# Scores of two heads by 64-row matmuls in two halves of the TensorE array, without zero-padded copies

## The chip, the cores and the metric

The kernel runs on one core of a Trainium2 chip. The metric is the device time of one execution in microseconds (us). Ratios are the mean time of one kernel's fast runs over that of the kernel before in the same rounds, so they are not quite the ratio of the medians quoted beside them.

## The reference, cut to what matters

```python
# 4 sequences, 8 heads, 768 tokens, head dimension 48
for t in range(S):
    cur = einsum('bhd,bhe->bhde', u * k_t, v_t)
    y[:, :, t] = einsum('bhd,bhde->bhe', r_t, state + cur)
    state = w * state + einsum('bhd,bhe->bhde', k_t, v_t)
# then: x = y as [batch, token, head*dim]; each token goes to one of 8 experts
# (768x384 per sequence, hidden size 1024, relu), scaled by its gate
```

The recurrence is computed in chunks of 128 tokens. Inside a chunk, the term between tokens s < t is a score (r_t w^t)(k_s w^-(s+1)); what came before the chunk enters through a state. All data are float32.

## The kernel before

Two heads form a pair and fill the 128 partitions as 2 x 64 rows (48 of data, 16 of padding). There are 16 pairs: 4 sequences of 4. For a pair, `first` computes the state increments (`ds`), the scores (`sc`) and the token's own term (`dp`); `second`, which follows one pair later, computes the output (`yp`). At each fourth pair, `finish` turns the outputs (`tp`) and computes the logits (`lp`, `lq`).

```python
DP = 64                # rows that a head takes
rbs = [once.tile([P, NCH, 2, P], F32, name=f"rb{i}") for i in range(2)]   # zeroed in the other head's part
...
# first(n, hp, t)
nc.gpsimd.tensor_mul(rw, t["rT"], spread(pw[:, hp, :P], 1, NCH))
for i in range(2):                                    # the padded copies
    q = slice(i * DP, (i + 1) * DP)
    nc.scalar.copy(rb[q, :, i, :], rw[q])
nc.vector.tensor_mul(kw, t["kT"], spread(inv[:, hp], 1, NCH))
nc.gpsimd.tensor_mul(ke, t["k"], spread(endT[:, hp], 1, NCH))
nc.gpsimd.tensor_mul(pd, t["rT"], t["kT"])
ds = [bank("ds") for _ in range(2)]                   # 5 matmuls 128x128x128
...
for c in range(NCH - 1):                              # the state chain: VectorE, head by head
    for i in range(2):
        ...                                           # copy for c == 0, else state = w^128 state + ds
for g in range(0, NCH, 2):                            # scores
    sc = bank("sc")
    for c in range(2):
        nc.tensor.matmul(sc[:, c * 2 * P:(c + 1) * 2 * P], lhsT=kw[:, g + c, :],
                         rhs=rb[:, g + c].rearrange("p i t -> p (i t)"), start=True, stop=True)
    nc.vector.tensor_mul(am[:, g:g + 2]..., sc..., spread(mask, 1, 4))
...                                                   # dp and own; second() comes one pair later
```

`rw`, `kw`, `ke`, `pd`, `am` and `own` have two buffers each; all PSUM tiles go round through eight banks.

## Time and profile before

| | us |
|---|---|
| median of the runs before the prediction | 600.85 |
| attention (to the last logits) | 213 |
| routing and experts | 386 |
| one sequence of four pairs | 49.0 |

How the pairs are bounded is read in the prediction. Besides the lines there, three groups of the page matter: line, engine, operation, count, then busy us, mean ns, and the idle time of the engine before it with what ended it.

```profile
L138 PE MATMUL sc<-rb,kw 128*128 128x256 f32 x192 | 48.7, 406 | 22.7 <-ACT rb L112 22.7
...
L112 ACT COPY rb<-rw 64x768 f32<-64x768 f32 x32 | 26.6, 831 | 122.1 <-POOL rw L109 121.8
...
L140 DVE TENSOR_TENSOR am<-sc,mask 128x512 f32<-128x512 f32 x48 | 32.8, 691 | 9.9 <-PE sc L138 9.0
```

The 96 score matmuls are 192 records, since a float32 matmul is two. They hold TensorE for 48.7 us, and half of the products are with zeros. The 22.7 us of idle time ahead of them are the wait for the ScalarE copies.

### The profile page before, as it was taken

To read this page: it belongs to the slowest core of one execution; us is meant where nothing else is said; L and a number is where in the kernel's file an instruction comes from. 1 tells how busy PE (TensorE), PEld (TensorE's weight loads), DVE (VectorE), ACT (ScalarE), POOL (GpSimd) and SP (SyncE) were. 2 spreads that over 40 slices of the span, in tenths; PEclk is the share of its full clock that TensorE was granted. 3 is DMA by queue.
4 is the path that set the end of the run, shared out by engine and by line. 5 is a ranking of instruction groups with operands and counts; after the bars stand their busy time and mean duration, and the time that the engine had idled before them with its cause. 6 is when DMAs were issued, how large, how long until landed. Compare 5 with 4: busy or idle time off the path is not lost. (4 is left out here: it accounts for less than half of the span.)

```text
span 599.1 us, 8255 instructions
## 1 busy us (share of the span) xinstructions
PE 527.1 (88%) x3283; PEld 415.3 (69%) x3283; DVE 187.8 (31%) x433; ACT 79.6 (13%) x128; POOL 162.6 (27%) x140
## 2 busy tenths in 40 slices
PE   0888898898797933699999999999999999999994
PEld 0766656657666712588787887877878878778783
DVE  6796647738736347001101110111011101110010
ACT  1121211131222100011011010110110101101010
POOL 5964526434622011311121211211112112110010
PEclk9998999999999975599999999999999999999998
DMA  8686464654420115658999999988989899998830
GB/s 303 244 288 214 159 208 155 241 161 155 127 85 28 36 47 217 254 187 310 332 332 310 329 323 341 319 321 323 332 325 321 318 335 303 337 324 324 313 127 0
DMA packets 28411, 145.39 MB, mean 243 GB/s; under 512 B 4336, under 2 KB 7439, under 8 KB 20432
## 3 DMA queue, kind: packets, MB, share of 16 engines
q1 hardware_dynamic: 20448, 128.98, 61.2%
q0 software_dynamic: 3968, 10.82, 4.8%
q10 hardware_dynamic: 3952, 5.00, 2.3%
q8 instruction: 28, 0.46, 0.3%
q14 instruction: 15, 0.12, 0.1%
HBM read 135.35 MB, written 10.81 MB: 244 GB/s over the span
## 5 line engine op out<-in xcount | busy, mean ns | idle before, releaser
L490 PEld LDWEIGHTS hps<-exT,w1t 128*128 128x128 f32 x1488 | 173.0, 194 | 9.0 <-DVE exT L481 1.1
L490 PE MATMUL hps<-exT,w1t 128*128 128x128 f32 x1488 | 173.3, 277 | 0.6 <-DVE exT L481 0.6
L498 PE MATMUL eyp<-w2t,hT 128*128 128x384 f32 x496 | 165.1, 486 | 0.0
L498 PEld LDWEIGHTS eyp<-w2t,hT 128*128 128x128 f32 x496 | 91.8, 190 | 57.5
L492 ACT ACTIVATE hT<-hps 128x512 f32<-128x512 f32 x62 | 37.0, 597 | 331.4 <-PE hps L490 331.4
L502 POOL DMA_INDIRECT out_dram<-yo,sid x31 | 31.2, 1007 | 174.8 <-DVE yo L501 174.8
L138 PE MATMUL sc<-rb,kw 128*128 128x256 f32 x192 | 48.7, 406 | 22.7 <-ACT rb L112 22.7
L481 DVE COPY exT<-etp 128x384 f32<-128x384 f32 x31 | 17.3, 558 | 160.4 <-PE etp L479 160.4
L501 DVE TENSOR_SCALAR yo<-eyp,gate 128x384 f32<-128x384 f32 x31 | 19.1, 618 | 148.1 <-PE eyp L498 148.1
L471 POOL DMA_INDIRECT xg<-x_d,gid x31 | 30.6, 987 | 121.8 <-PE etp L479 107.3
L138 PEld LDWEIGHTS sc<-rb,kw 128*128 128x128 f32 x192 | 37.5, 202 | 30.4 <-ACT rb L112 25.3
L115 POOL TENSOR_TENSOR pd<-rT,kT 128x768 f32<-128x768 f32 x16 | 35.7, 2233 | 49.4 <-PE dp L148 38.0
L112 ACT COPY rb<-rw 64x768 f32<-64x768 f32 x32 | 26.6, 831 | 122.1 <-POOL rw L109 121.8
L130 DVE SCALAR_TENSOR_TENSOR st<-st,pw,ds 64x64 f32<-64x64 f32 x128 | 35.9, 280 | 4.1
L109 POOL TENSOR_TENSOR rw<-rT,pw 128x768 f32<-128x768 f32 x16 | 27.2, 1703 | 35.2 <-PE yp L159 35.2
L140 DVE TENSOR_TENSOR am<-sc,mask 128x512 f32<-128x512 f32 x48 | 32.8, 691 | 9.9 <-PE sc L138 9.0
L114 POOL TENSOR_TENSOR ke<-k,endT 128x768 f32<-128x768 f32 x16 | 29.1, 1818 | 6.2 <-DVE endT L93 3.0
L165 PE MATMUL yp<-am,v 128*64 128x128 f32 x384 | 29.3, 281 | 0.0
L120 PE MATMUL ds<-v,ke 128*128 128x128 f32 x160 | 23.1, 294 | 3.0 <-POOL ke L114 3.0
L159 PEld LDWEIGHTS yp<-rw,st 128*128 128x128 f32 x160 | 21.2, 191 | 6.2 <-issue 2.9
L159 PE MATMUL yp<-rw,st 128*128 128x128 f32 x160 | 25.1, 288 | 0.0
L120 PEld LDWEIGHTS ds<-v,ke 128*128 128x128 f32 x160 | 20.2, 200 | 6.1 <-POOL ke L114 3.4
(130 smaller groups left out, 278.5 us busy)
## 6 DMA issues: line engine op xcount, KB each, us to landing
w1t<-in_w_dram SPq DMA_DIRECT2D x31, 1536.0 KB
w2t<-in_w_dram SPq DMA_DIRECT2D x31, 1536.0 KB
rT<-in_rT_dram SPq DMA_DIRECT2D x16, 384.0 KB
kT<-in_kT_dram SPq DMA_DIRECT2D x16, 384.0 KB
k<-in_k_dram SPq DMA_DIRECT2D x16, 384.0 KB
v<-in_v_dram SPq DMA_DIRECT2D x16, 384.0 KB
vT<-in_vT_dram SPq DMA_DIRECT2D x16, 384.0 KB
x_d<-x ACTq DMA_DIRECT2D x4, 1152.0 KB
```

The source lines that it names most:

```text
L115: nc.gpsimd.tensor_mul(pd, t["rT"], t["kT"])
L120: nc.tensor.matmul(ds[c // 3][:, c % 3 * P:(c % 3 + 1) * P], lhsT=ke[:, c, :], rhs=t["v"][:, c, :], start=True, stop=True)
L130: nc.vector.scalar_tensor_tensor(state[q, c, i], state[q, c - 1, i], pw[q, hp, P:P + 1], add, Alu.mult, Alu.add)
L138: nc.tensor.matmul(sc[:, c * 2 * P:(c + 1) * 2 * P], lhsT=kw[:, g + c, :], rhs=rb[:, g + c].rearrange("p i t -> p (i t)"), start=True, sto ...
L140: nc.vector.tensor_mul(am[:, g:g + 2].rearrange("p c i t -> p (c i) t"), sc.rearrange("p (x t) -> p x t", t=P), spread(mask, 1, 4))
L159: nc.tensor.matmul(yp[:, c % 3 * P:(c % 3 + 1) * P], lhsT=t["state"][:, c - 1].rearrange("p i e -> p (i e)"), rhs=t["rw"][:, c, :], start= ...
L165: nc.tensor.matmul(yp[i * DP:(i + 1) * DP, c % 3 * P:(c % 3 + 1) * P], lhsT=t["v"][:, c, i * DP:(i + 1) * DP], rhs=t["am"][:, c, i, :], st ...
L471: nc.gpsimd.indirect_dma_start(out=xg, out_offset=None, in_=x_d, in_offset=bass.IndirectOffsetOnAxis(ap=gid[:, j:j + 1], axis=0))
L490: nc.tensor.matmul(hps[:, m * P:(m + 1) * P], lhsT=t[j]["w1"][:, 4 * g + m, kk, :], rhs=t[j]["xT"][:, kk, :], start=(kk == 0), stop=(kk == ...
L492: nc.scalar.activation(hT[:, 4 * g:4 * g + 4].rearrange("p m t -> p (m t)"), hps, Act.Relu)
L498: nc.tensor.matmul(yp[:, :D], lhsT=t[j]["hT"][:, m, :], rhs=t[j]["w2"][:, m, :], start=(m == 0), stop=(m == FK - 1))
L502: nc.gpsimd.indirect_dma_start(out=out, out_offset=bass.IndirectOffsetOnAxis(ap=sid[:, j:j + 1], axis=0), in_=yo, in_offset=None, bounds_c ...
```

## The change

The intent is to stop multiplying zeros. Each head's scores come from its own 64 rows, in its half of the array, so that both run at once; then no padded copy of `rw` is needed.

```diff
-        rbs = [once.tile([P, NCH, 2, P], F32, name=f"rb{i}") for i in range(2)]
...
-        for z in rbs + sts:
+        for z in sts:
...
-            for i in range(2):
-                q = slice(i * DP, (i + 1) * DP)
-                nc.scalar.copy(rb[q, :, i, :], rw[q])
...
-            t["am"] = am = two.tile([P, NCH, 2, P], F32, name="am")
-            for g in range(0, NCH, 2):
-                sc = bank("sc")
-                for c in range(2):
-                    nc.tensor.matmul(sc[:, c * 2 * P:(c + 1) * 2 * P], lhsT=kw[:, g + c, :],
-                                     rhs=rb[:, g + c].rearrange("p i t -> p (i t)"), start=True, stop=True)
-                nc.vector.tensor_mul(am[:, g:g + 2].rearrange("p c i t -> p (c i) t"),
-                                     sc.rearrange("p (x t) -> p x t", t=P), spread(mask, 1, 4))
+            t["am"] = am = two.tile([P, 2, NCH, P], F32, name="am")
+            for g in range(0, NCH, 3):
+                sc = [bank("sc") for _ in range(2)]
+                for c in range(3):
+                    for i in range(2):
+                        q = slice(i * DP, (i + 1) * DP)
+                        nc.tensor.matmul(sc[i][:, c * P:(c + 1) * P], lhsT=kw[q, g + c, :],
+                                         rhs=rw[q, g + c, :], start=True, stop=True)
+                for i in range(2):
+                    nc.vector.tensor_mul(am[:, i, g:g + 3], sc[i][:, :3 * P].rearrange("p (c t) -> p c t", t=P),
+                                         spread(mask, 1, 3))
...
-                                         lhsT=t["v"][:, c, i * DP:(i + 1) * DP], rhs=t["am"][:, c, i, :],
+                                         lhsT=t["v"][:, c, i * DP:(i + 1) * DP], rhs=t["am"][:, i, c, :],
```

More of the change, by code (lines that the diff above doesn't have):

```diff
@@ L106, in first @@
             pd = two.tile([P, NCH, P], F32, name="pd")
-            rb, state = rbs[n % 2], sts[n % 2]
+            state = sts[n % 2]
             t.update(rw=rw, state=state)
             nc.gpsimd.tensor_mul(rw, t["rT"], spread(pw[:, hp, :P], 1, NCH))
-            for i in range(2):
-                q = slice(i * DP, (i + 1) * DP)
-                nc.scalar.copy(rb[q, :, i, :], rw[q])
             nc.vector.tensor_mul(kw, t["kT"], spread(inv[:, hp], 1, NCH))
```

## The prediction

> **What bounds the kernel now.** I read the page first (busy shares, then the 40 slices). The kernel has two stages: attention up to 213 us, experts from about 235 us on. The change touches attention alone, so I cut the trace into stretches by time.
>
> ```profile
> PE 527.1 (88%) x3283; PEld 415.3 (69%) x3283; DVE 187.8 (31%) x433; ACT 79.6 (13%) x128; POOL 162.6 (27%) x140
> ```
>
> TensorE leads overall, but that is an average over both stages. The stretches below are one whole sequence (four pairs of heads) and two single pairs, from one `ds` block to the next:
>
> ```profile
> 83.06:132.08 49.02, 42.52 (x288) 31.74 (x287) 31.10 (x73) 10.24 (x16) 23.29 (x13) 1.00 0.55 185
> 132.08:141.82 9.74, 8.38 (x63) 6.77 (x61) 7.72 (x18) 1.66 (x2) 5.51 (x4) 1.00 0.39 123
> 141.82:152.00 10.18, 8.38 (x63) 6.77 (x61) 7.72 (x18) 1.66 (x2) 5.95 (x4) 1.00 0.49 164
> ```
>
> The columns are PE, weight loads, VectorE, ScalarE, GpSimd, clock, DMA share, GB/s. A pair takes 10.18 us, TensorE works 8.38 us of it and VectorE 7.72: TensorE is the bound, VectorE is close behind, DMA and ScalarE are far from it. The 1.80 us in which TensorE rests are one wait, which the view of waits of TensorE for the stage shows and the timeline explains:
>
> ```profile
> PE sc L138 <- ACT rb L112: 22.7, 14, 2.0
> ...
> PE ds L120 <- POOL ke L114: 3.0, 1, 3.0
> ```
>
> ```profile
> 141.41 1.83 POOL L109 TENSOR_TENSOR rw<-rT,pw 128x768 f32<-128x768 f32 x1
> ...
> 141.82 1.38 PE L120 MATMUL ds<-v,ke 128*128 128x128 f32 x10
> ...
> 143.27 1.67 ACT L112 COPY rb<-rw 64x768 f32<-64x768 f32 x2 [8.51 <-POOL rw L109]
> ...
> 145.00 2.86 PE L138 MATMUL sc<-rb,kw 128*128 128x256 f32 x12 [1.80 <-ACT rb L112]
> ...
> 147.69 1.45 PE L148 MATMUL dp<-pd,uz 128*128 128x384 f32 x4
> ...
> 151.19 0.88 PE L165 MATMUL yp<-am,v 128*64 128x128 f32 x12
> ```
>
> See that `rw` ends at 143.24, when `ds` has just ended (143.20); the two ScalarE copies into the padded tile then take 1.67 us, and TensorE waits for exactly these. The wait falls in 14 of the 16 pairs.
>
> **What the Trainium skill says.** (1) "TensorEngine Tiling (Array Packing)", Key Properties: tiles of the array run weight loads and matmuls in parallel, and a change of tiling mode (not of tile) drains TensorE. The trace agrees for column tiles: the `yp` matmuls of 64 columns (L165) against full ones (L159):
>
> ```profile
> L165 PE MATMUL yp<-am,v 128*64 128x128 f32 x324 | 24.9, 281 | 0.0
> L159 PE MATMUL yp<-rw,st 128*128 128x128 f32 x140 | 21.9, 287 | 0.0
> L165 PEld LDWEIGHTS yp<-am,v 128*64 128x64 f32 x324 | 17.7, 136 | 3.3
> ```
>
> Each record lasts the same (281 and 287 ns), but 24.9/324 = 77 ns of busy time go to one of L165 and 21.9/140 = 156 to one of L159: two at a time. Each switch back to the full array shows as about 0.17 us of "issue" before the next weight load. (2) "TensorE: Matmul & The Clock Gate", Part 3: small-K matmuls on separate row groups run together. No row tile runs in the kernel before, so its trace can't confirm this. (3) The same page, section LDWEIGHTS: the time of a weight load goes with its columns, not its rows. This matters: the new loads have 64 rows but still 128 columns, and there are twice as many. (4) The tiling page, Gotcha 1: row tiles must write different PSUM banks; the diff does this with `sc[0]` and `sc[1]`.
>
> **The change part by part.** The compiled order of instructions on TensorE is the same as before apart from the score block, so terms may be added per pair.
>
> (a) *The copies go.* 32 ScalarE copies of 831 ns leave, and scores depend on `rw` directly. In the pair shown, scores could start at 143.24 plus some 0.1 us of signalling in place of 145.00. `rw` starts 0.4 us before `ds` does and takes 1.55 to 2.19 us, mean 1.69, so I leave a wait of 0.2 us per pair, now on GpSimd: 14 x 0.2 = 2.8. Saved: 22.7 - 2.8 = 19.9 us.
>
> (b) *The score matmuls.* Now 6 matmuls per pair (12 records, as each f32 matmul is two) stream 256 columns, half of whose products are with zeros; block start to next block start is 147.69 - 145.00 = 2.69 us. After, 12 matmuls of 64 rows and 128 columns (24 records). The nearest thing measured is L165: 6 matmuls of 128 columns in two tiles, from 151.19 to the next block at 152.00, so 0.81 us with one switch of 0.17, or 0.64 of work. Twelve take 2 x 0.64, and the block now has a switch on both sides (`ds` and `dp` use the full array): 1.28 + 0.34 = 1.62 us. Saved: 16 x (2.69 - 1.62) = 17.1 us. This rests on row tiles overlapping as column tiles do.
>
> (c) *The mask.* Three VectorE products of 512 (691 ns each, about 0.63 back to back) become four of 384; `own` has that shape and takes about 0.50 us back to back. 4 x 0.50 - 3 x 0.63 = +0.1 us per pair, off TensorE's path.
>
> (d) *Banks.* Scores take four PSUM banks per pair in place of three, of eight that go round. An allocation waits for the one eight before it; counting ten per pair in place of nine, `dp` now waits for the `xT` additions of the pair before, the second half of the scores for `own`.
>
> (e) *Start.* The padded tiles' zeroing (3.0 us on GpSimd) goes, but the compiled order puts two `rw` and two `pd` ahead of the first `ke` on GpSimd, and `ke` waits for a VectorE table anyway. Gain about zero.
>
> (f) *VectorE as the next bound.* TensorE's pair becomes 8.38 - 1.07 + 0.2 = 7.5 us. VectorE has 7.72 + 0.1 = 7.8 busy, with gaps nearer 8.2: it falls behind by about 0.7 us a pair. But each fourth pair holds TensorE 9 us longer (49.0 - 4 x 8.38 - 6.5 of waits: transposes and logits), where VectorE has almost nothing and catches up. Setting the blocks of one sequence against each other by hand with these durations, VectorE is about 2 us behind at the end of the third pair, and the releases in (d) come just in time or up to 1 us late. I give back 1 us per sequence, 4 us.
>
> Sum: 19.9 + 17.1 - 4 = 33 us, all from attention. 600.85 - 33 = 568 us (ratio 0.945).
>
> **The rivals.**
> - *Row tiles do not load weights in parallel.* Then 24 loads at the spacing that `ds` shows (1.38 us for 10 records with a 0.28 tail, about 0.11 each) take 2.7 us, plus 0.34 of switches, and (b) turns into a loss of 0.3 us x 16 = 5 us. Only (a) stays: 600.85 - 19.9 + 5 = 586. For it: (3) above and doubled loads. Against it: loads of the two column tiles already overlap: 324 of 136 ns lie in 17.7 us, 2.5 at a time. I give it 15%.
> - *VectorE becomes the full bound.* If all three pairs between the logits blocks run at 8.2 to 8.5 us in place of 7.5, some 3 us per sequence are given back, in place of 1: 576. For it: 7.72 us busy already, and GpSimd's products slow VectorE's when both run (`kw` takes 0.95 to 1.75 us). Against it: the catch-up in every fourth pair.
> - *The wait only changes its name.* If `rw` came later, the scores would wait for GpSimd as they do for ScalarE. GpSimd is busy 5.95 of 10.18 us and `rw` waits for the previous-but-one pair's state matmuls on TensorE, which keep their place 0.8 us ahead of `ds`; so this wait can't grow much. At 1 us per pair it would cost 11 us more: 579.
> - *Clock.* In the slice from 45 us the page's granted clock is 0.8, and the score block at 45.30 us took 4.54 us where others take 2.86. One such stretch more or less moves the total by about 2 us either way.
>
> **Range and chances.** Everything working, without giving back, is 600.85 - 37 = 564, and a warm start could bring 2 more: low end 561. The high end, 580, holds the rivals on VectorE and on the wait; serial weight loads lie beyond it. "Faster by over 2%" means under about 589 us; even the serial case is at 586. So 0.93 faster, 0.06 same, 0.01 slower.
>
> **What would show each step.** (a): the wait of `sc` is named after GpSimd's `rw` and sums to about 3 us. (b): the score block from its start to the start of `dp` is 1.6 us, and its 384 records take about 26 us busy or less in place of 48.7; if it is 2.7 to 3, loads are serial. (c): `am` x64 of about 0.55 us. (f): VectorE's share near 95% in the pairs without logits, and new waits of `dp` or `sc` on VectorE of about 1 us per sequence. One sequence takes 40 us in place of 49.0, and experts take the same 386 us after attention. I am wrong if attention shrinks by less than 20 us, or if the experts' stage moves.

## The result, and the profile after

The changed kernel takes 569.83 us (median of 4, 569.43 to 570.42) against 600.84 us: ratio 0.9483, 95% interval 0.9451 to 0.9514. The profiled execution spans 568.7 us against 599.1. Attention ends at about 182 us in place of 213; the rest takes 386 us in both. So the whole gain is attention's.

The page of the changed kernel: the engines, then the score matmuls, the mask and the weight loads of the scores.

```profile
PE 510.6 (90%) x3475; PEld 399.7 (70%) x3475; DVE 189.2 (33%) x449; ACT 53.5 (9%) x96; POOL 158.6 (28%) x136
...
L140 DVE TENSOR_TENSOR am<-sc,mask 128x384 f32<-128x384 f32 x64 | 31.2, 550 | 0.5
L137 PE MATMUL sc<-rw,kw 64*128 64x128 f32 x384 | 27.1, 290 | 2.3 <-POOL rw L108 2.3
...
L137 PEld LDWEIGHTS sc<-rw,kw 64*128 64x128 f32 x384 | 23.9, 196 | 4.4 <-POOL rw L108 2.6
```

Twice as many score records take 27.1 us in place of 48.7. Their 384 weight loads of 196 ns each would be 75 us one after another; they lie in 23.9, so 3.1 are under way at a time. Loads of the full array overlap as well (160 loads of `ds`, 200 ns each, lie in 20.2 us), but 1.6 at a time: the doubling is the two halves loading side by side. The matmuls do the same: in the pair shown below, the first records of the two halves start at 83.31 and 83.32 us. As the prediction's point (3) has it, a load of 64 rows is no shorter than one of 128: 196 ns here, 202 ns before.

Stretches of time, with the columns of the prediction: three pairs in a row, then the sequence they belong to.

```profile
115.21:122.47 7.26, 7.26 (x74) 5.90 (x73) 6.52 (x18) 0.00 (x0) 5.18 (x4) 1.00 0.54 165
122.47:130.32 7.85, 7.49 (x74) 5.82 (x72) 7.53 (x18) 0.00 (x0) 5.83 (x4) 1.00 0.54 200
130.32:138.17 7.85, 7.50 (x74) 5.82 (x72) 7.53 (x21) 0.00 (x0) 5.83 (x4) 1.00 0.46 152
115.21:155.69 40.48, 39.06 (x336) 27.95 (x334) 31.42 (x77) 3.76 (x8) 22.15 (x13) 1.00 0.43 147
```

The first pair after a logits block takes 7.26 us and TensorE is busy all of it. The next two take 7.85 us, and now VectorE is full: 7.53 us, and the other 0.32 us are gaps of about 0.03 us between the instructions of its state chain. The view of TensorE's waits in attention, us in total, times, longest:

```profile
PE sc L137 <- POOL rw L108: 2.3, 2, 1.7
PE tp L176 <- DVE st L126: 1.8, 3, 0.6
PE yp L159 <- DVE st L126: 1.4, 4, 0.4
PE ds L116 <- DMA v<-in_v_dram: 0.3, 1, 0.3
```

Waits for ScalarE are gone. What is new are waits of the outputs and of the transposes for the state chain on VectorE. These matmuls need no result of that chain; they wait for a PSUM bank that it still reads. (This is read from the order of allocation: ten banks are taken per pair, so the first bank of `yp`, or of `tp` after a fourth pair, is the one that this pair's `ds` took eight allocations earlier.) The timeline of one pair shows how VectorE falls behind:

```profile
81.41 1.82 POOL L108 TENSOR_TENSOR rw<-rT,pw 128x768 f32<-128x768 f32 x1 [0.30 <-PE yp L159]
81.52 2.52 DVE L109 TENSOR_TENSOR kw<-kT,inv 128x768 f32<-128x768 f32 x1
...
83.31 1.61 PE L137 MATMUL sc<-rw,kw 64*128 64x128 f32 x24
...
83.96 1.01 DVE L168 TENSOR_TENSOR xT<-yp,own 128x384 f32<-128x384 f32 x2
84.85 0.94 PEld L148 LDWEIGHTS dp<-pd,uz 128*128 128x128 f32 x4
...
84.89 0.47 DVE L124 COPY st<-ds 64x64 f32<-64x64 f32 x2
85.39 2.47 DVE L126 SCALAR_TENSOR_TENSOR st<-st,pw,ds 64x64 f32<-64x64 f32 x8
...
86.75 0.68 PE L159 MATMUL yp<-rw,st 128*128 128x128 f32 x4 [0.35 <-DVE st L126]
```

The scores' block starts at 83.31 and the next (`dp`) at 84.85: 1.54 us in place of 2.69. From `dp` to `yp` it is 1.90 us, where 1.40 is usual, because the chain that frees the bank ends late. And `kw` lasts 2.52 us. It was issued just after GpSimd's `rw` and ended 0.81 us after it. The Trainium skill states why, on its page "SBUF — State Buffer", section "Who interferes with whom": a VectorE instruction with two SBUF inputs contends with a GpSimd instruction that reads SBUF, and whichever was issued first has the shared port for the whole instruction. The trace agrees, both ways round. In a pair of the kernel before, `kw` was issued first; it took 0.95 us, and GpSimd's `pd` beside it 2.35 us, where it takes 1.81 us in the run with three buffers described below, in which it starts first:

```profile
149.01 0.95 DVE L113 TENSOR_TENSOR kw<-kT,inv 128x768 f32<-128x768 f32 x1
149.28 2.35 POOL L115 TENSOR_TENSOR pd<-rT,kT 128x768 f32<-128x768 f32 x1 [4.14 <-PE dp L148]
```

In the steady sequence of the changed kernel the four `kw` take 2.53, 1.20, 0.95 and 0.95 us, in that of the kernel before 0.95 us each: 1.8 us of VectorE's time. No run changed the order of issue alone, so what this costs is not shown.

### The profile page after: what moved, and what is told of

It is laid out like the page before. It is cut to its first block, busy times and chain, and to the rows that moved or that the text cites. A ratio compares the mean times of both kernels' runs of the same rounds, so it can differ in the third digit from the quotient of the medians.

```text
span 568.7 us, 8584 instructions
## 1 busy us (share of the span) xinstructions
PE 510.6 (90%) x3475; PEld 399.7 (70%) x3475; DVE 189.2 (33%) x449; ACT 53.5 (9%) x96; POOL 158.6 (28%) x136
## 5 line engine op out<-in xcount | busy, mean ns | idle before, releaser
L108 POOL TENSOR_TENSOR rw<-rT,pw 128x768 f32<-128x768 f32 x16 | 28.8, 1798 | 42.8 <-PE yp L159 42.0
L111 POOL TENSOR_TENSOR pd<-rT,kT 128x768 f32<-128x768 f32 x16 | 29.7, 1858 | 17.1 <-PE dp L148 13.1
L110 POOL TENSOR_TENSOR ke<-k,endT 128x768 f32<-128x768 f32 x16 | 32.3, 2021 | 7.0 <-POOL rw L108 2.5
L140 DVE TENSOR_TENSOR am<-sc,mask 128x384 f32<-128x384 f32 x64 | 31.2, 550 | 0.5
L137 PE MATMUL sc<-rw,kw 64*128 64x128 f32 x384 | 27.1, 290 | 2.3 <-POOL rw L108 2.3
L137 PEld LDWEIGHTS sc<-rw,kw 64*128 64x128 f32 x384 | 23.9, 196 | 4.4 <-POOL rw L108 2.6
L116 PEld LDWEIGHTS ds<-v,ke 128*128 128x128 f32 x160 | 20.2, 200 | 9.4 <-POOL ke L110 6.4
L148 PE MATMUL dp<-pd,uz 128*128 128x384 f32 x64 | 25.5, 521 | 0.0
```

Source lines behind the costliest of these rows:

```text
L116: nc.tensor.matmul(ds[c // 3][:, c % 3 * P:(c % 3 + 1) * P], lhsT=ke[:, c, :], rhs=t["v"][:, c, :], start=True, stop=True)
L137: nc.tensor.matmul(sc[i][:, c * P:(c + 1) * P], lhsT=kw[q, g + c, :], rhs=rw[q, g + c, :], start=True, stop=True)
L140: nc.vector.tensor_mul(am[:, i, g:g + 3], sc[i][:, :3 * P].rearrange("p (c t) -> p c t", t=P), spread(mask, 1, 3))
```

## The experiments

All eleven kernels gave the correct result and were timed in three rounds beside the kernel before, whose medians were 600.47, 600.94 and 600.87 us. A "sequence" is the time of four pairs in the steady part, as in the fences above.

| kernel | a steady pair | a sequence | median us | ratio |
|---|---|---|---|---|
| before | 10.18 | 49.00 | 600.84 | 1 |
| three buffers, old scores | 8.11 | 41.44 | 576.65 | 0.9607 |
| new scores, copies kept | 9.29 | 45.32 | 594.76 | 0.9915 |
| **changed** | 7.26, 7.85 | 40.48 | 569.83 | 0.9483 |
| changed, by heads | 7.58, 8.14 | 40.28 | 572.69 | 0.9531 |
| changed, first copies on ScalarE | 7.34 | 38.93 | 568.21 | 0.9443 |
| changed, third `rw` buffer | | 40.12 | 569.73 | 0.9472 |
| changed, zeroing kept | 7.85 | 40.45 | 567.30 | 0.9430 |
| changed, compact states | 7.60 | 38.34 | 564.98 | 0.9404 |
| compact, third `rw` buffer | 6.61 | 35.21 | 551.68 | 0.9169 |
| the same, first `ke` on VectorE | 6.60 | 35.22 | 551.30 | 0.9163 |

### Part (a) alone: the copies without their wait

```diff
-        rbs = [... for i in range(2)]
+        rbs = [... for i in range(3)]
-            rw = two.tile([P, NCH, P], F32, name="rw")
+            rw = three.tile([P, NCH, P], F32, name="rw")     # a pool of three buffers
-            rb, state = rbs[n % 2], sts[n % 2]
+            rb, state = rbs[n % 3], sts[n % 2]
```

> The kernel before with three buffers in place of two for the decayed r and for its padded copy, so that neither has to wait for the matmuls of the pair before the last; the scores themselves are as before. Theory: the wait for the ScalarE copies (22.7 us) is a matter of when the copies may start, and part (a) of the change is worth it all alone: 600.8 - 20 = 581 us, score blocks still 2.7 us, no wait of the scores on ScalarE in the steady pairs, a pair of 8.4 us. Rival: the chain rw -> copy -> scores only gets another name (GpSimd too busy): over 590 us.

It took 576.65 us (interval of the ratio 0.9585 to 0.9629): the theory holds, and the gain, 24 us, is larger than the 20 expected. One pair and one sequence:

```profile
82.85:90.96 8.11, 8.11 (x62) 6.69 (x60) 7.67 (x19) 1.66 (x2) 5.77 (x4) 1.00 0.78 241
116.19:157.63 41.44, 41.44 (x288) 31.44 (x286) 31.10 (x73) 10.25 (x16) 22.30 (x13) 1.00 0.44 134
```

The copies are still made (1.66 us of ScalarE per pair), but a pair ahead, and TensorE doesn't pause at all in the sequence. The wait was worth 10.18 - 8.11 = 2.07 us per pair, not the 1.80 that the view of waits showed. The rest is in the matmuls' own rows: from `ds` to the scores it is 1.22 us here, while the page before counts 1.38 us for `ds`, because the last matmul ahead of a wait shows its whole tail, and the first after it its weight load (the score block shrinks from 2.69 to 2.59 us).

### Part (b) alone: the new scores with the copies kept

```diff
+            rc = two.tile([P, NCH, P], F32, name="rc")
+            for i in range(2):
+                q = slice(i * DP, (i + 1) * DP)
+                nc.scalar.copy(rc[q], rw[q])
...
-                                         rhs=rw[q, g + c, :], start=True, stop=True)
+                                         rhs=rc[q, g + c, :], start=True, stop=True)
```

> The changed kernel with the two ScalarE copies put back (into an unpadded tile that the 64-row score matmuls read). Part (b) alone. Theory: the wait of about 1.7 us per pair comes back, the score block stays at 1.5 us: 570 + 20, less what VectorE gave back, so about 583 us, and VectorE causes no wait. Rival (parts not additive, the wait is absorbed by a slack that the shorter score block makes): under 576 us.

It took 594.76 us: 12 us over the 583 of my theory, and further from the rival's 576. The timeline of a pair shows the first cause:

```profile
94.67 1.68 ACT L112 COPY rc<-rw 64x768 f32<-64x768 f32 x2 [7.62 <-POOL rw L108]
95.55 2.46 PE L141 MATMUL sc<-rc,kw 64*128 64x128 f32 x24 [1.12 <-ACT rc L112]
```

The wait is split in two. The first head's scores start after the first copy, the second head's must wait for the second, within the block, which takes 2.46 us in place of 1.61 (it is not in the named wait of 1.12 us). A pair takes 9.29 us: 2.03 more than 7.26. So the sequence gains 49.00 - 45.32 = 3.7 us, four times that 14.7. The other losses lie outside the steady part: the first `ds` starts at 19.12 us in place of 16.52, and two pairs near the start (12.39 and 11.24 us) fell into stretches of lower clock (0.86 and 0.85 on average), where the profile before shows one (12.05 us against 10.18). Of the some 3 us that this leaves between the medians, 1.05 is that the profiled run (593.71 us) was faster than the median, and 0.7 lies after attention (386.7 against 385.9 us); the cause of the rest is open. In the steady part the account is clear: a sequence gains 7.6 us by (a) alone and 3.7 by (b) alone, 11.2 together, but the changed kernel gains 8.5. So 2.7 us per sequence are given back where both parts are in; the next section but one asks by what. The theory's total, 583 us, was missed.

### Does the order of the two heads matter?

```diff
-                for c in range(3):
-                    for i in range(2):
+                for i in range(2):
+                    for c in range(3):
```

> The changed kernel with the score matmuls of a bank group ordered by head (three of head 0, then three of head 1) in place of alternating. Same matmuls, loads, banks and masks. Theory: two row tiles overlap only when neighbours in the order lie in different row groups, so only one boundary in each group of six overlaps: the score block grows from 1.54 to about 2.5 us, a pair to about 8.2 us, VectorE's waits go: about 580 us. Rival (TensorE finds the overlap whatever the order): 570 us.

It took 572.69 us (0.9506 to 0.9557, which overlaps the changed kernel's interval). My theory missed: the block grew to 1.93 us only. The matmuls and loads of the score block of one pair, first for its start, then all of it (duration min/median/max, first and last start):

```profile
L137 PE MATMUL sc<-rw,kw x4: 272/322/373, 77.3 to 77.6; 64*128 64x128 f32 x4
```

```profile
L137 PE MATMUL sc<-rw,kw x24: 272/272/373, 77.3 to 79.0; 64*128 64x128 f32 x24
```

The queue holds three matmuls (six records) of head 0, then three of head 1, and so on. The trace has the first starts at 77.30, 77.51, 77.62 and 77.63 us. Records of one half start 0.11 us apart (0.21 after the first), so the fourth belongs to the other half: head 1 starts while half of head 0's six records have yet to start (they do so from 77.74 to 77.96 us). All 24 take 1.93 us; one after another at 0.11 they would take 2.7. TensorE finds most of the overlap whatever the order. And the 0.32 us more per block are free in the steady part, as VectorE sets the pace there (40.28 us per sequence, against 40.48).

### Is VectorE what was given back?

The two copies that begin a pair's state chain go to ScalarE, which is idle:

```diff
-                        nc.vector.tensor_copy(state[q, 0, i], add)
+                        nc.scalar.copy(state[q, 0, i], add)
```

> The changed kernel with the two copies that begin a pair's state chain (0.47 us of VectorE per pair) on the idle ScalarE. Theory: VectorE's load of 7.85 us a pair is what is given back (2.4 us per sequence over four pairs of 7.26 us); with 0.5 us less, the pairs that now take 7.85 come down towards 7.3 to 7.4, 4 to 6 us in all: 564 to 567 us. Rival: the banks or GpSimd hold these pairs: 569 or more.

```profile
122.01:129.35 7.34, 7.34 (x74) 5.82 (x72) 7.08 (x16) 0.41 (x2) 5.84 (x4) 1.00 0.64 214
129.35:136.69 7.34, 7.34 (x74) 5.82 (x72) 7.08 (x18) 0.41 (x2) 5.85 (x4) 1.00 0.49 163
```

The pairs that took 7.85 us take 7.34: they lost 0.51 us, just what VectorE's copies took with their gaps, while TensorE's work stayed the same. So VectorE paced them. (TensorE is now busy in all of the 7.34 us, so they could hardly fall further.) The sequence comes down by 1.55 us; the rest of what was given back is not shown to be VectorE's. The total came down only by 1.6 us to 568.21, over the 564 to 567 expected and with overlapping intervals (0.9397 to 0.9489): the profile has a low-clock stretch at 36 us and a 1.9 us wait for `kw` near the start.

The other direction adds one VectorE product of 128x384 per pair, its result unused, to both kernels:

```diff
+            junk = two.tile([P, 3, P], F32, name="junk")
+            nc.vector.tensor_mul(junk, t["vT"][:, :3], t["vT"][:, :3])
```

> The changed kernel with one more VectorE product of 128x384 per pair (about 0.45 us, its result unused). Theory: VectorE is the bound of about two pairs in four (7.85 us a pair), so its time comes through there and in part in the others: 16 x 0.45 = 7 us at most, 3 to 7 us expected, 573 to 577 us. Rival: VectorE is not the bound and what holds TensorE is the number of banks: 570.

> The kernel before with the same additional VectorE product per pair. Theory: there VectorE has 2.4 us free in a pair of 10.2, so nothing comes through: 600 to 602 us. Rival: every VectorE instruction counts in both kernels: 604 or more.

They took 579.58 us (0.9628) and 606.86 us (1.0101), both above what I expected; by its total alone, the second would fit the rival (604 or more). The product costs more than 0.45 us, as it takes two SBUF inputs and queues behind GpSimd (895 and 1114 ns on average), and it sometimes waits for a load. The steady pairs tell the theories apart. First two pairs of the changed kernel with the addition (it fell into the second only), then one of the kernel before with it:

```profile
127.23:135.08 7.85, 7.50 (x74) 5.82 (x72) 7.53 (x18) 0.00 (x0) 5.84 (x4) 1.00 0.58 200
135.08:144.54 9.46, 7.76 (x74) 5.74 (x72) 9.14 (x21) 0.00 (x0) 5.80 (x4) 1.00 0.36 126
```

```profile
144.60:154.77 10.17, 8.38 (x62) 6.76 (x60) 8.71 (x19) 1.66 (x2) 5.93 (x4) 1.00 0.52 163
```

In the changed kernel VectorE's busy time rose by 9.14 - 7.53 = 1.61 us and the pair by 9.46 - 7.85 = 1.61. In the kernel before it rose from 7.72 to 8.71, and the pair stayed at 10.17. The 6 us that the latter lost are elsewhere: its profile has two low-clock stretches in place of one and its first `ds` begins at 19.03 us.

Each of these edits also moves the end of the state chain, and with it the release of the `ds` banks, so they don't part VectorE's load from the lateness of its chain. That VectorE has no idle time left in these pairs, beyond the gaps inside the chain, speaks for the load.

### The start, and a third buffer for `rw`

Putting the zeroing of the (now unused) padded tiles back delays GpSimd by 3 us, and with it goes back the compiled order of its first products:

```diff
+        rbs = [once.tile([P, NCH, 2, P], F32, name=f"rb{i}") for i in range(2)]
-        for z in sts:
+        for z in rbs + sts:
```

> The changed kernel with the zeroing of the padded tiles put back (3 us of GpSimd at the start, the tiles unused), which also brings back the order of GpSimd's first products (ke first, two rw and pd later). Theory: the first state increments begin at about 16.5 us again in place of 18.9, and 1 to 2 us of it reach the end: 568 to 569 us. Rival: the change of order is worth nothing: 570 us or more.

The first `ds` begins at 16.63 us in place of 18.90, the last logits come at 179.05 in place of 181.99, and the total is 567.30 us. The steady sequence is unchanged.

What I had expected as the reason, a queue of two `rw` and two `pd` ahead of the first `ke`, does not hold. The first `ds` needs `ke`, but GpSimd had done these and stood idle for 1.50 us, until VectorE had copied out the table (`endT`) that `ke` reads. The table comes after the first two `kw`. First the kernel before (the run with the zeroing has the same durations, 0.11 us later), then the changed kernel:

```profile
12.18 1.81 DVE L113 TENSOR_TENSOR kw<-kT,inv 128x768 f32<-128x768 f32 x2
13.91 0.68 DVE L93 COPY endT<-ep 128x512 f32<-128x512 f32 x1
```

```profile
11.60 4.77 DVE L109 TENSOR_TENSOR kw<-kT,inv 128x768 f32<-128x768 f32 x2
16.29 0.68 DVE L92 COPY endT<-ep 128x512 f32<-128x512 f32 x1
```

The two `kw` take 4.77 us beside GpSimd's second `rw` and `pd`; in the other order GpSimd has no product to make during that time, and they take 1.81. The table comes 2.38 us later, and so does the first `ds`. So the removal of useless work cost about 2 us here, by the order that it led to, through the same collision of `kw` with GpSimd as in the steady pairs. The intervals of the two ratios overlap slightly (0.9386 to 0.9474 against 0.9451 to 0.9514), so the total alone would not prove it.

The third buffer is the first edit's `three.tile` line for `rw`, in the changed kernel:

> The changed kernel with three buffers in place of two for rw. Its scores wait for rw only twice, 2.3 us in all, near the start. Theory: with VectorE as the bound of its steady pairs, a third buffer brings those 2 us at most: 567 to 569 us (while it brought 13 us with the compact states). Rival: rw's time of start also sets VectorE's speed (its product kw runs beside it), 565 or less.

569.73 us: no difference (0.9429 to 0.9515), where I had expected up to 2 us. The waits for `rw` are gone from its profile, but 1.2 us of waits for `kw` stand in their place.

### A version that beats both

The states are stored compactly: with the increments of the two heads computed in two halves of the array's columns, into the partitions where each head's state lies, one VectorE instruction updates both heads, one bank holds all increments, and the states need no zeroing.

```diff
-            ds = [bank("ds") for _ in range(2)]
+            ds = bank("ds")
             for c in range(NCH - 1):
-                nc.tensor.matmul(ds[c // 3][:, ...], lhsT=ke[:, c, :], rhs=t["v"][:, c, :], ...)
+                for i in range(2):
+                    q = slice(i * DP, (i + 1) * DP)
+                    nc.tensor.matmul(ds[q, c * DP:(c + 1) * DP], lhsT=ke[:, c, q], rhs=t["v"][:, c, q], ...)
...
-                        nc.vector.scalar_tensor_tensor(state[q, c, i], state[q, c - 1, i], pw[q, hp, P:P + 1], ...)
+                    nc.vector.scalar_tensor_tensor(state[:, c], state[:, c - 1], pw[:, hp, P:P + 1], ...)
...
-                        nc.tensor.matmul(yp[:, ...], lhsT=t["state"][:, c - 1]..., rhs=t["rw"][:, c, :], ...)
+                        for i in range(2):
+                            nc.tensor.matmul(yp[q, ...], lhsT=t["state"][q, c - 1], rhs=t["rw"][q, c, :], ...)
```

> The changed kernel with the states compact: the state increments of the two heads by 64-column matmuls in two halves of the array into one bank (no cross products), so that one VectorE instruction over 128 rows updates both heads (5 in place of 10 per pair), and the state term of y by 64x64 tiles. Theory: what is given back in the changed kernel, 2.4 us per sequence, is VectorE's (7.85 us per pair), and VectorE drops to about 6.5 us: no wait on the state chain, pairs bound by TensorE at 6.7 to 7.3 us: 550 to 560 us. Rival: the give-back has another cause, the pairs stay at 7.8: 565 or more.

564.98 us, over the theory's 550 to 560: the waits for the state chain are gone, but a pair takes 7.60 us, not 6.7 to 7.3. (The edit changes VectorE's work, the banks and TensorE's matmuls at once, so it doesn't single out one of them.) The stretch of one pair, and the wait that now leads:

```profile
81.28:88.88 7.60, 6.68 (x97) 5.09 (x94) 6.82 (x15) 0.00 (x0) 5.70 (x4) 1.00 0.85 257
```

```profile
PE sc L132 <- POOL rw L104: 11.6, 14, 2.4
```

`ds` has become so short (0.75 us in place of 1.38) that GpSimd's `rw`, which starts when the state matmuls of the pair before the last have read the other buffer, is no longer hidden behind it. This is the prediction's third rival, one step later. A third buffer for `rw`, worth nothing in the changed kernel, is now the remedy:

> The run with compact states, with three buffers in place of two for the decayed r (rw). There, the scores waited for GpSimd's rw, 0.92 us in most pairs (11.6 us in all), because rw may only start when the state matmuls of the pair before the last are done and the block of state increments that had hidden it is shorter. Theory: this wait goes and the pair comes down from 7.60 to 6.7 to 6.9 us, where VectorE (6.8 busy) and TensorE (6.7) are both full: 565 - 11 = 554 us. Rival: GpSimd's own work (5.7 us a pair) or VectorE holds the pair at 7.3 or more: over 560 us.

```profile
74.51:81.12 6.61, 6.61 (x97) 5.10 (x94) 6.50 (x15) 0.00 (x0) 5.75 (x4) 1.00 0.87 267
```

551.68 us (0.9138 to 0.9199): TensorE is busy throughout, and VectorE has 6.50 of 6.61 us. Last, the first pair's `ke` by VectorE, ahead of GpSimd's queue:

```diff
-            nc.gpsimd.tensor_mul(ke, ...)
+            (nc.gpsimd if n else nc.vector).tensor_mul(ke, ...)
```

> As a_compact_rw3, and the first pair's product ke by VectorE in place of GpSimd, so that it doesn't queue behind two pairs' rw and pd. Theory: in the changed kernel the first state increments begin at 18.9 us and not at 16.5 because of that queue; now at about 16: 2 to 3 us under a_compact_rw3, so about 551 us. Rival: the start is hidden by something else (loads, the cold clock): no difference.

551.30 us, no difference that the intervals show (0.9131 to 0.9194). The first `ds` came at 18.16 us in place of 19.12, not at 16: this `ke`, too, had to wait for the table, which VectorE copied out at 16.43 us after 4.77 us of `kw`.

## Why the prediction was right

The time (568 predicted, 569.83 measured) was right, and so were the cause and the place. But three terms were off in size, and they cancelled: that the number came within 2 us is partly luck.

- **What bounds a pair, and (a).** Right in kind, too small. I took the wait as the 1.80 us in the view and left 0.2 us per pair for `rw`: 19.9 us. The run with three buffers shows 2.07 us per pair and 24 us in all, and in the changed kernel `rw` holds the scores only twice, for 2.3 us in all. I had not counted that a wait also lengthens the rows beside it.
- **(b), the score matmuls.** The overlap of row tiles is as assumed: the block takes 1.54 us against 1.62 predicted (its records hold TensorE for 27.1 us, about 26 forecast), and the rival of serial weight loads is out. The term was too large because the 2.69 us of before held 0.10 us of the wait, and because the switches also lengthen the neighbours: against the run with three buffers, `ds` to scores grew from 1.22 to 1.31 us and `dp` to `yp` from 1.29 to 1.40. Net 8.11 - 7.26 = 0.85 us per pair, 13.6 us over 16 pairs, in place of 17.1. The argument against the rival was weaker than it reads: 2.5 loads at a time were set against one, while loads of the full array in the same trace already ran 1.6 at a time (150 of 200 ns in 19.0 us).
- **(c), the mask.** Right: 550 ns each, and the four take 1.95 us back to back, where the three of before took 1.89 in the run with three buffers.
- **(d) and (f), banks and VectorE.** This is the term that was off most. The mechanism is as described, VectorE falling behind and banks being released late, and the VectorE experiments show VectorE's part in it; VectorE's share of the pairs without logits, 7.53 of 7.85 us, is the 95% or so forecast. The size is not: without it, a sequence would take the 41.44 us of three buffers less 4 x 0.85, that is 38.0; it takes 40.48. So 2.4 us per sequence were given back, not 1 (2.7 by the run with the copies kept); of these, the copies on ScalarE brought 1.55 back. Two things were missed: `kw` slows down beside GpSimd (1429 ns on average in the changed kernel's attention against 1097 before), and the waits fall on `yp` and `tp`, for the banks of `ds`, not on `dp` and the scores. By the prediction's own rule, that an allocation waits for the one eight before it, `yp` should have been on its list.
- **(e), the start.** Predicted zero, because `ke` waits for VectorE's table in either order. But the order delays the table: the first `ds` came 2.4 us later, and the run with the zeroing put back recovers it. In return the changed kernel's profile has no low-clock stretch in attention, where the one before lost 1.9 us to one; nothing shows that this is due to the change.
- **One sequence.** Predicted 40 us, measured 40.48. Part (a) brings 49.00 - 41.44 = 7.6 of the difference of 8.5, part (b) 3.4. The 2.4 that are given back were taken as what is left, so that this sum closes proves nothing.

Three points stay open: about 1 us of the run with the copies kept; why the head-by-head run's profile is 2.5 us longer than the changed kernel's (1.0 us lies after attention, 387.1 against 386.1, and 1.6 in the first two sequences, none in the steady part); and the 0.9 us per sequence that are given back and that the copies on ScalarE did not bring back.

## What to carry to other kernels

Before removing work to remove a wait, ask whether one more buffer removes it: here it brought 24 of the 31 us alone, and 7.6 of the 8.5 us of a steady sequence; the new matmuls added little on top, since the next engine was close behind. When the bound engine gets faster, sum the next engine's busy time over one period and count what it shares with a neighbour; if hardly any of the period is left (here 0.32 of 7.85 us), lighten it in the same change. A pause can cost more than the view of waits names (here 2.07 us, not 1.80), because the rows on either side of it hold a part.

## What the Trainium skill lacked or had wrong

- "TensorEngine Tiling (Array Packing)", Key Properties, says that a change of tiling mode drains TensorE but gives no size. Here, with a block of row tiles between two full-array blocks, `ds` to scores took 0.09 us and `dp` to `yp` 0.11 us longer than with a full-array block.
- "TensorE: Matmul & The Clock Gate", Part 3, has matmuls strictly in program order in start and end. With the heads queued three by three, a record of head 1 started at 77.63 us, before the last three of head 0's six (77.74 to 77.96 us), which stand ahead of it in the queue; 24 records took 1.93 us where 0.11 us each would be 2.7. Alternating the tiles gave 1.61 us. (The profile models the ends of matmuls, so it says nothing on their order.)
- The same page tells of weight loads overlapping in-flight matmuls of other row groups; that the loads of two row tiles also overlap each other, which decides this change, is said outright only in the tiling page's general sentence. Here 384 loads of 196 ns lay in 23.9 us, 3.1 at a time, against 1.6 for the full-array loads of `ds`.
